# Two transformer layers on one core: the weights' preparation issued by Pool, and exponentials on VectorE in all heads of the first layer

## The chip, the cores and the metric

One core of a Trainium2 chip runs the whole program in a single launch. The metric is device time in microseconds (us); several timed runs give a median, and one further execution is recorded by the profiler. The engines are TensorE (PE, with its weight loads as PEld), VectorE (DVE), ScalarE (ACT), GpSimd (Pool) and SyncE (SP). Each works through its own instructions in order and waits on semaphores; SP, ACT and Pool can begin DMA transfers from their queues.

## The reference

Attention and a gated feed-forward block alternate, twice, with the same weights in both layers:

```
x: 2048 x 448, 16 heads of 28, feed-forward width 1792
for layer in 0, 1:
    q, k, v = layernorm(x) @ wqkv                      # per head 2048 x 28 each
    x = x + concat_h(softmax(q k^T * 28**-0.5) v) @ wo
    z = layernorm(x)
    x = x + (sigmoid(z @ w_gate) * (z @ w_up)) @ w_down
```

All inputs and the output are float32.

## The kernel before, in words

Every float32 matrix is cut into a high and a low float16 part, and products are sums of part products. In layer 0 the parts of `wqkv` are made at the start. The parts of `wo`, `w_gate`, `w_up` and `w_down` are made during the attention of layer 0 by the class `Prepare` (L715) and written to DRAM tensors `o_parts`, `gu_parts`, `dn_parts`; both layers load them from there afterwards.

**Attention** (`attend`, L831). The score matrix of a head, transposed, has 16 chunks of 128 keys by 4 blocks of 512 queries: 64 units of 128x512 per head, 1024 per layer. `score(g)` (L860) takes the next three units of the list `main`: TensorE writes their scores into a triple of PSUM banks (tile `sc`, L856; four matmuls per unit), and one ScalarE instruction at L871 turns all three into exponentials (tile `prob`, ring of six). This is called a group here. `mix` (L897, matmuls at L907) multiplies exponentials by the values into the accumulator `acc`, a PSUM bank that alternates with the head: `bank(h % 2, "acc")`. It goes chunk by chunk, each chunk in four quarters. When the last chunk of a head is mixed, `finish(h)` (L928) has VectorE copy the accumulator to `oraw` (L933), take the reciprocal of the denominators (L935), scale and cut into parts; SP then sends the parts to the tiles `ot` (L951, L953).

**Units aside.** The units in `side` are not in `main`. Their scores go into one PSUM bank of their own (tile `aside`), and VectorE computes their exponential with a polynomial of ten instructions (`score_aside`, L873, chain L881 to L890). The bank is that of the other accumulator: `bank(1 - h % 2, "aside")`, so it comes free when `oraw` of the previous head has been copied. In layer 0 only heads 10 to 15 have such units, two each (begun at chunks 4 and 9 of the head); in layer 1 all heads have two.

**Order.** It is written out by hand. The loop over groups (L986) emits `more(g)` (the next group, and at the third chunk of a head the loads of head `h + 2`: a memset by VectorE at L467 and six transfers by SP, L471 to L478), then a unit aside if one is due, then as many quarters of `mix` as `due` says. When a chunk `c` of the layer (0 to 255) has been mixed, `along(c)` (L919) may emit one step of the preparation.

**The preparation.** It has twelve tiles: one of `wo`, four of `w_down`, seven of `w_gate` with `w_up`. Twelve steps measure the tiles (VectorE sums squares, L773, L775), one step (`sizes`, L787) turns the sums into powers of two with a Pool reduction, twelve steps cut the tiles again (VectorE at L189 and L194) and the last one writes what is left. Each step first begins the read of the next tile (L171 to L174 in `load_rows`, or L744), then the write of the parts cut by the step before (L766), and then emits the VectorE work on its own tile. A gate/up tile needs six reads. All of these transfers are begun by SP. The tiles `raw`, `junk` and `pack` come from `big`, a first-in first-out list of free slots that the head operands `qp`, the outputs `ot` and others draw on too; a slot that is taken again makes its new writer wait for its old readers.

```
            if prepare and prepare.steps and c > 4 and c % 6 == 0:
                prepare.steps.popleft()()
```

So a step is emitted every six chunks, from chunk 6 to chunk 156, which is in head 9.

Of the kernel before, what the change touches and what calls it, by code (L numbers as in the profile page):

```python
# [12 lines left out]
BF16 = mybir.dt.bfloat16  # L13
F16 = mybir.dt.float16
# [5 lines left out]
P = 128  # L20
S = 2048
D = 448
H = 16
DH = 28
F = 1792
NT = S // P
NB = 4
# [61 lines left out]
def interleaved_layers(ctx: ExitStack, tc: tile.TileContext, x_in, wqkv, wo, w_gate, w_up,  # L89
                       w_down, out):  # L90
    nc = tc.nc
# [6 lines left out]
    big = Slots(spool, "s", N_SLOTS)  # L98
# [26 lines left out]
    x = cpool.tile([P, NT, D], F32, name="x")  # L125
# [40 lines left out]
    qrt.put(ind_f)  # L166


    def load_rows(dst, src, c0, n):

        nc.sync.dma_start(dst[:, 0:3, :],  # L171
                          src[0:384, c0:c0 + n].rearrange("(s p) n -> p s n", p=P))
        nc.sync.dma_start(dst[0:64, 3, :], src[384:448, c0:c0 + n])
        nc.sync.dma_start(dst[64:128, 3, :], src[384:448, c0:c0 + n])  # L174

    def split(hi, lo, raw):

        nc.scalar.copy(hi, raw)  # L178
        nc.vector.tensor_tensor(lo, raw, hi, op=ALU.subtract)  # L179
# [223 lines left out]
    o_parts = dpool.tile([P, 2, 4, D], F16, name="o_parts")  # L403
    gu_parts = dpool.tile([NF // 2, P, 2, 2, 4, 2 * P], F16, name="gu_parts")
    dn_parts = dpool.tile([4, P, 4, 2, D], F16, name="dn_parts")

    class WeightsQKV:
# [307 lines left out]
    class Prepare:  # L715


        def __init__(self):
            nc.vector.memset(sums[:, 3:7], 0.0)
            self.part = cpool.tile([P, 2], F32, name="part", tag="part", bufs=1)  # L720
            self.at = 0
            tiles = [("o", 0)] + [("d", j) for j in range(4)] + [("gu", j) for j in range(7)]
            self.read(*tiles[0])
            self.steps = deque()
            for do in (self.measure, self.split):
                for i, what in enumerate(tiles):
                    last = do == self.split and i == len(tiles) - 1
                    self.steps.append(lambda do=do, what=what, then=None if last else
                                      tiles[(i + 1) % len(tiles)]: self.step(do, what, then))
                if do == self.measure:  # L730
                    self.steps.append(self.sizes)
            self.steps.append(self.write)
            self.pack = None

        def read(self, kind, j):
            self.next = big.get("raw", [P, 2048])
            if kind == "o":
                load_rows(self.view(self.next, kind), wo, 0, D)
            elif kind == "gu":
                for i, w in enumerate((w_gate, w_up)):  # L740
                    load_rows(self.view(self.next, kind)[:, i], w, j * 2 * P, 2 * P)
            else:
                n = self.count(j)
                nc.sync.dma_start(self.view(self.next, kind)[:, 0:n, :],  # L744
                                  w_down[j * 512:j * 512 + n * P, :].rearrange(
                                      "(s p) n -> p s n", p=P))

        def count(self, j):
            return min(4, NF - 4 * j)
# [6 lines left out]
        def step(self, do, what, then):  # L756
            raw = self.next
            if then:
                self.read(*then)
            self.write()  # L760
            do(raw, *what)
            big.put(raw)

        def write(self):
            if self.pack:
                nc.sync.dma_start(*self.pack[0:2])  # L766
                big.put(self.pack[2])
                self.pack = None

        def add(self, m, v):  # L770
            junk = big.get("junk", [P, 2048], BF16)
            n = v.free_size()
            nc.vector.tensor_tensor_reduce(junk[:, 0:n], v, v, 1.0, sums[:, m:m + 1],  # L773
                                           op0=ALU.mult, op1=ALU.add, accum_out=self.part[:, 0:1])
            nc.vector.tensor_copy(sums[:, m:m + 1], self.part[:, 0:1])  # L775
            big.put(junk)

        def measure(self, raw, kind, j):
            if kind == "o":
# [16 lines left out]
        def split(self, raw, kind, j):  # L796
            v = self.view(raw, kind)
            if kind == "o":
                t = big.get("pack", [P, 2, 4, D], F16)
                scaled_split(t[:, 0], t[:, 1], v, 3, nc.vector)  # L800
                self.pack = (o_parts, t, t)
            elif kind == "gu":
                t = big.get("pack", [P, 2, 2, 4, 2 * P], F16)
                for w in range(2):
                    scaled_split(t[:, w, 0], t[:, w, 1], v[:, w], 4 + w, nc.vector)
                self.pack = (gu_parts[j], t, t)
            else:
                n = self.count(j)
                t = big.get("pack", [P, 4, 2, D], F16)
                scaled_split(t[:, 0:n, 0], t[:, 0:n, 1], v[:, 0:n], 6, nc.vector)  # L810
                self.pack = (dn_parts[j][:, 0:n], t[:, 0:n], t)

    class Outputs:

# [16 lines left out]
    def attend(layer, values, heads, last_values, gate, keep):  # L831
# [3 lines left out]
        prepare = None  # L835
# [4 lines left out]


        side = {}
        free_from = 10 if layer == 0 else 0
        for h in range(free_from, H):
            for at, kc, qb in ((4, 10, 3), (9, 15, 1)):
                side[(h * NT + at) * NB] = (h * NT + kc) * NB + qb
        main = [u for u in range(units) if u not in side.values()]
        groups = (len(main) + 2) // 3
# [70 lines left out]
        def along(c):  # L919
            nonlocal prepare  # L920
            if layer == 0 and c == 2:
                keep()
            if layer == 0 and c == 4:
                prepare = Prepare()
            if prepare and prepare.steps and c > 4 and c % 6 == 0:
                prepare.steps.popleft()()

        def finish(h):  # L928
            acc = accs.pop(h)
# [49 lines left out]


        quarters, i, done = 4 * total, 0, 0
        alone = main.index(free_from * NT * NB) // 3
        pace = (quarters + len(side) - 3 * alone) / (groups - alone)
        for g in range(2, groups + 3):
            more(g)
            x = g - 2.25  # L986
            due = int(3 * x if x < alone else 3 * alone + (x - alone) * pace)
            if g >= groups:
                due = 2 * quarters
            if begin:  # L990
# [68 lines left out]
    def gated(layer, first, wt, before_next):  # L1059
# [33 lines left out]
        for b, p in seq:  # L1093
# [113 lines left out]
```

## Time and profile before

| | |
|---|---|
| median of 3 runs | 2001.17 us (1999.59 to 2002.54) |
| the profiled execution: its time, its span | 2000.05 us, 1998.3 us |
| PE, DVE, ACT, POOL busy | 1965.6, 1003.4, 1167.3, 33.5 us |
| mean granted TensorE clock | 0.996 |
| exponentials of layer 0: first to last start at L871 | 126.1 to 591.8 us, 338 instructions |
| exponentials of layer 1: first to last start at L871 | 1124.1 to 1568.2 us, 331 instructions |

Busy time is what the profiler records for instructions; PE's is modelled and is near the whole span in every stage, so it does not tell where TensorE is short of time. The two stretches with exponentials take 910 of the 1998 us; between and after them come the projections and the feed-forward blocks, which the change does not touch.

### The profile page before, as it was taken

The numbers are of one execution on the slowest core, as the hardware profiler recorded it, in microseconds if no ns is written. First come the engines' busy times: TensorE is split into PE (matmuls) and PEld (weight loads), VectorE is DVE, ScalarE is ACT, GpSimd is POOL, SyncE is SP. The second block draws the span as 40 slices with busy tenths as digits, with TensorE's granted clock in tenths as the row PEclk, the third lists the DMA queues.
The fourth block names the chain that finished last, engine by engine and source line by source line (L and its number), as shares of the span: only waits on it lengthen the run. The fifth ranks groups of instructions, "written<-read, shape, count | busy, mean of one in ns | idle before, by whom it ended". The sixth has DMA issues, their size and how long they took to land. (4 is left out here: it accounts for less than half of the span.)

```text
span 1998.3 us, 48079 instructions
## 1 busy us (share of the span) xinstructions
PE 1965.6 (98%) x21549; PEld 1001.7 (50%) x21549; DVE 1003.4 (50%) x1551; ACT 1167.3 (58%) x1129; POOL 33.5 (2%) x76
## 2 busy tenths in 40 slices
PE   9999999979999999999999999999999999999999
PEld 4445555545554444444444555555555544444444
DVE  6634545477664323333255477677776732323222
ACT  5569999979981211121235699999999412121211
POOL 2000000000000000000000000000000000000000
PEclk9999999989999999999999999999999999999999
DMA  4563544751016101010234311111111250101000
GB/s 166 161 208 84 149 124 152 224 146 43 17 51 233 37 1 37 1 38 1 92 94 140 100 48 32 48 49 44 46 34 51 68 196 11 56 1 56 0 19 19
DMA packets 98633, 153.77 MB, mean 77 GB/s; under 512 B 9584, under 2 KB 79216, under 8 KB 95600
## 3 DMA queue, kind: packets, MB, share of 16 engines
q1 hardware_dynamic: 89728, 146.21, 23.9%
q10 hardware_dynamic: 8688, 4.36, 0.9%
q8 instruction: 173, 2.83, 0.6%
q14 instruction: 44, 0.36, 0.1%
HBM read 97.52 MB, written 45.68 MB: 72 GB/s over the span
## 5 line engine op out<-in xcount | busy, mean ns | idle before, releaser
L871 ACT ACTIVATE prob_s<-sc 128x1536 f32<-128x1536 f32 x669 | 898.4, 1562 | 15.4 <-PE sc L856 13.0
L907 PE MATMUL acc<-prob_s,val_s 128*32 128x256 f32 (+3 forms) x7938 | 568.1, 381 | 0.0
L856 PE MATMUL sc<-qp_s 114*32 114x512 f16 x8016 | 557.8, 380 | 3.2 <-ACT val_s L567 1.3
L1116 ACT ACTIVATE sig_q<-gate 128x512 f32<-128x512 f32 x112 | 60.8, 595 | 597.4 <-PE up L386 597.4
L856 PEld LDWEIGHTS <-qp_s 114*32 114x32 f16 x8192 | 247.6, 95 | 251.9 <-issue 142.8
L907 PEld LDWEIGHTS acc<-prob_s,val_s 128*32 128x32 f32 x7938 | 263.2, 110 | 155.1 <-issue 9.7
L1117 DVE SCALAR_TENSOR_TENSOR sig_q<-up,sig_q 128x512 f32<-128x512 f32 x112 | 72.1, 686 | 513.8 <-ACT sig_q L1116 513.8
L1080 PE MATMUL dnp<-dn_s,hhl_q 128*128 128x448 f16 x448 | 158.4, 354 | 0.0
L1081 PE MATMUL dnp<-dn_s,hhl_q 128*128 128x448 f16 x448 | 157.9, 352 | 0.0
L1082 PE MATMUL dnp<-dn_s,hhl_q 128*128 128x448 f16 x448 | 157.9, 352 | 0.0
L372 PE MATMUL qkp<-xhl_s,wqk_s 128*128 128x512 f16 x616 | 139.6, 379 | 2.6 <-ACT xhl_s L178 0.9
L379 PE MATMUL gate<-xhl_s,gu_s 128*128 128x512 f16 x336 | 127.3, 379 | 3.4 <-ACT xhl_s L178 2.5
L380 PE MATMUL gate<-xhl_s,gu_s 128*128 128x512 f16 x336 | 127.3, 379 | 1.4 <-DVE xhl_s L179 1.4
L381 PE MATMUL up<-xhl_s,gu_s 128*128 128x512 f16 x336 | 127.3, 379 | 0.0
L380 PE MATMUL up<-xhl_s,gu_s 128*128 128x512 f16 x336 | 127.3, 379 | 0.0
L379 PE MATMUL up<-xhl_s,gu_s 128*128 128x512 f16 x336 | 127.3, 379 | 0.0
L381 PE MATMUL gate<-xhl_s,gu_s 128*128 128x512 f16 x336 | 127.3, 379 | 0.0
L933 DVE COPY oraw_q<-acc 128x512 f32<-128x512 f32 x32 | 22.1, 692 | 179.1 <-PE acc L907 179.0
L935 DVE RECIPROCAL oden_q<-oden_q 128x512 f32<-128x512 f32 x32 | 107.3, 3353 | 1.1
L380 PEld LDWEIGHTS <-gu_s 128*128 128x128 f16 x672 | 65.7, 98 | 81.3 <-issue 3.9
L381 PEld LDWEIGHTS <-gu_s 128*128 128x128 f16 x672 | 65.7, 98 | 81.3 <-issue 2.5
L379 PEld LDWEIGHTS <-gu_s 128*128 128x128 f16 x672 | 65.7, 98 | 79.0 <-issue 1.7
(139 smaller groups left out, 1900.8 us busy)
## 6 DMA issues: line engine op xcount, KB each, us to landing
qp_s<-qk_scr SPq DMA_DIRECT2D x96, 224.0 KB
qk_scr<-qkhl_q SPq DMA_DIRECT2D x56, 256.0 KB
gu_s<-gu_parts SPq DMA_DIRECT2D x14, 1024.0 KB
xraw_s<-xt_scr SPq DMA_DIRECT2D x14, 768.0 KB
xt_scr<-xs_s SPq DMA_DIRECT2D x38, 224.0 KB
qp_s<-qk_scr SPq DMA_DIRECT2D x64, 112.0 KB
gu_parts<-pack_s SPq DMA_DIRECT2D x7, 1024.0 KB
raw_s<-in_B_w_down_dram SPq DMA_DIRECT2D x6, 896.0 KB
```

What stands on the lines that cost most here:

```text
L372: nc.tensor.matmul(pm, w, x, start=(i == 0), stop=(i == len(terms) - 1))
L379: nc.tensor.matmul(pm, wh(o, kt), blk.hi[:, kt, :], start=(kt == 0), stop=False)
L380: nc.tensor.matmul(pm, wh(o, kt), blk.lo[:, kt, :], start=False, stop=False)
L381: nc.tensor.matmul(pm, wl(o, kt), blk.hi[:, kt, :], start=False, stop=False)
L856: nc.tensor.matmul(ps[32 * j:32 * j + 32, :], hd.k[:, keys], hd.q[:, qb * W:(qb + 1) * W], start=True, stop=True, tile_position=(0, 32 * j))
L871: nc.scalar.activation(prob[:, 0:n, :], ps[:, 0:n, :], AF.Exp, scale=exp_scale)
L907: nc.tensor.matmul(acc[qb * VC:(qb + 1) * VC, s], v[:, kc % TB, h, :], probs[c * NB + qb][:, s], start=(kc == 0 and a == 0), stop=(kc == N ...
L935: nc.vector.reciprocal(den, den)
L1080: nc.tensor.matmul(pm, hl[:, 0, s], dw[:, 0, :], start=(f == 0), stop=False)
L1081: nc.tensor.matmul(pm, hl[:, 0, s], dw[:, 1, :], start=False, stop=False)
L1082: nc.tensor.matmul(pm, hl[:, 1, s], dw[:, 0, :], start=False, stop=(f == NF - 1))
L1117: nc.vector.scalar_tensor_tensor(sigs[a], pms[2 * a + 1], PS, sigs[a], op0=ALU.mult, op1=ALU.mult)
```

## The change

The reads and writes of the preparation are begun by Pool in place of SP. Its tiles come from two rings of their own, two slots for `raw` and two for `pack` and `junk`, taken from `big` at the start of the preparation and given back at its end. Its steps have due chunks: the measuring steps at chunks 6, 10, ... 50, `sizes` and the first cut at 54, the cuts at every sixth chunk up to 120, the last write at 126, in head 7. In layer 0 heads 0 to 8 get one unit aside each (begun at chunk 6 of the head, for key chunk 15), heads 9 to 15 two, as in layer 1. The pace of `mix` is worked out for the two parts.

```diff
-    def load_rows(dst, src, c0, n):
+    def load_rows(dst, src, c0, n, queue=nc.sync):
-        nc.sync.dma_start(dst[:, 0:3, :],
+        queue.dma_start(dst[:, 0:3, :],
...
     class Prepare:
-            self.at = 0
+            self.raws, self.packs = big.ring(2), big.ring(2)
             tiles = [("o", 0)] + [("d", j) for j in range(4)] + [("gu", j) for j in range(7)]
+            order = [(do, what) for do in (self.measure, self.split) for what in tiles]
...
+            at = 6
+            for i, (do, what) in enumerate(order):
+                then = order[i + 1][1] if i + 1 < len(order) else None
+                self.steps.append((at, lambda do=do, what=what, then=then:
+                                   self.step(do, what, then)))
+                at += 4 if do == self.measure else 6
+                if i == len(tiles) - 1:
+                    self.steps.append((at, self.sizes))
+            self.steps.append((at, self.end))
...
+        def along(self, c):
+            while self.steps and self.steps[0][0] <= c:
+                self.steps.popleft()[1]()
+
+        def end(self):
+            self.write()
+            big.free.extend(self.raws)
+            big.free.extend(self.packs)
...
-            self.next = big.get("raw", [P, 2048])
+            self.next = big.at(self.raws, "raw", [P, 2048])
             if kind == "o":
-                load_rows(self.view(self.next, kind), wo, 0, D)
+                load_rows(self.view(self.next, kind), wo, 0, D, nc.gpsimd)
...
         def write(self):
             if self.pack:
-                nc.sync.dma_start(*self.pack[0:2])
-                big.put(self.pack[2])
+                nc.gpsimd.dma_start(*self.pack)
                 self.pack = None
 
         def add(self, m, v):
-            junk = big.get("junk", [P, 2048], BF16)
+            junk = big.at(self.packs, "junk", [P, 2048], BF16)
...
-                t = big.get("pack", [P, 2, 4, D], F16)
+                t = big.at(self.packs, "pack", [P, 2, 4, D], F16)
...
     def attend(layer, values, heads, last_values, gate, keep):
-        free_from = 10 if layer == 0 else 0
-        for h in range(free_from, H):
-            for at, kc, qb in ((4, 10, 3), (9, 15, 1)):
+        both = 9 if layer == 0 else 0
+        for h in range(H):
+            for at, kc, qb in ((4, 10, 3), (9, 15, 1)) if h >= both else ((6, 15, 1),):
                 side[(h * NT + at) * NB] = (h * NT + kc) * NB + qb
...
-            if prepare and prepare.steps and c > 4 and c % 6 == 0:
-                prepare.steps.popleft()()
+            if prepare:
+                prepare.along(c)
...
-        alone = main.index(free_from * NT * NB) // 3
-        pace = (quarters + len(side) - 3 * alone) / (groups - alone)
+        few = both * NT * NB
+        turn = main.index(few) / 3
+        paces = (few + both) / max(turn, 1), (quarters + len(side) - few - both) / (groups - turn)
         for g in range(2, groups + 3):
             more(g)
             x = g - 2.25
-            due = int(3 * x if x < alone else 3 * alone + (x - alone) * pace)
+            due = int(min(x, turn) * paces[0] + max(x - turn, 0) * paces[1])
```

More of the change, by code (lines that the diff above doesn't have):

```diff
@@ L166, in interleaved_layers @@
     qrt.put(ind_f)
-    def load_rows(dst, src, c0, n):
[L171 to L174, printed above, removed]
+    def load_rows(dst, src, c0, n, queue=nc.sync):
+        queue.dma_start(dst[:, 0:3, :],
+                        src[0:384, c0:c0 + n].rearrange("(s p) n -> p s n", p=P))
+        queue.dma_start(dst[0:64, 3, :], src[384:448, c0:c0 + n])
+        queue.dma_start(dst[64:128, 3, :], src[384:448, c0:c0 + n])
     def split(hi, lo, raw):
@@ L720, in __init__ @@
             self.part = cpool.tile([P, 2], F32, name="part", tag="part", bufs=1)
-            self.at = 0
+            self.raws, self.packs = big.ring(2), big.ring(2)
             tiles = [("o", 0)] + [("d", j) for j in range(4)] + [("gu", j) for j in range(7)]
+            order = [(do, what) for do in (self.measure, self.split) for what in tiles]
             self.read(*tiles[0])
             self.steps = deque()
[L725 to L731, printed above, removed]
@@ L732, in __init__ @@
-            self.steps.append(self.write)
-            self.pack = None
+            at = 6
[6 more added lines that the diff above has]
+                    self.steps.append((at, self.sizes))
@@ L739, in read @@
             elif kind == "gu":
                 for i, w in enumerate((w_gate, w_up)):
-                    load_rows(self.view(self.next, kind)[:, i], w, j * 2 * P, 2 * P)
+                    load_rows(self.view(self.next, kind)[:, i], w, j * 2 * P, 2 * P, nc.gpsimd)
             else:
                 n = self.count(j)
-                nc.sync.dma_start(self.view(self.next, kind)[:, 0:n, :],
-                                  w_down[j * 512:j * 512 + n * P, :].rearrange(
-                                      "(s p) n -> p s n", p=P))
+                nc.gpsimd.dma_start(self.view(self.next, kind)[:, 0:n, :],
+                                    w_down[j * 512:j * 512 + n * P, :].rearrange(
+                                        "(s p) n -> p s n", p=P))
@@ L761, in step @@
             do(raw, *what)
-            big.put(raw)
         def write(self):
             if self.pack:
-                nc.sync.dma_start(*self.pack[0:2])
-                big.put(self.pack[2])
+                nc.gpsimd.dma_start(*self.pack)
                 self.pack = None
         def add(self, m, v):
-            junk = big.get("junk", [P, 2048], BF16)
+            junk = big.at(self.packs, "junk", [P, 2048], BF16)
             n = v.free_size()
@@ L775, in add @@
             nc.vector.tensor_copy(sums[:, m:m + 1], self.part[:, 0:1])
-            big.put(junk)
         def measure(self, raw, kind, j):
@@ L798, in split @@
             if kind == "o":
-                t = big.get("pack", [P, 2, 4, D], F16)
+                t = big.at(self.packs, "pack", [P, 2, 4, D], F16)
                 scaled_split(t[:, 0], t[:, 1], v, 3, nc.vector)
-                self.pack = (o_parts, t, t)
+                self.pack = (o_parts, t)
             elif kind == "gu":
-                t = big.get("pack", [P, 2, 2, 4, 2 * P], F16)
+                t = big.at(self.packs, "pack", [P, 2, 2, 4, 2 * P], F16)
                 for w in range(2):
                     scaled_split(t[:, w, 0], t[:, w, 1], v[:, w], 4 + w, nc.vector)
-                self.pack = (gu_parts[j], t, t)
+                self.pack = (gu_parts[j], t)
             else:
                 n = self.count(j)
-                t = big.get("pack", [P, 4, 2, D], F16)
+                t = big.at(self.packs, "pack", [P, 4, 2, D], F16)
                 scaled_split(t[:, 0:n, 0], t[:, 0:n, 1], v[:, 0:n], 6, nc.vector)
-                self.pack = (dn_parts[j][:, 0:n], t[:, 0:n], t)
+                self.pack = (dn_parts[j][:, 0:n], t[:, 0:n])
     class Outputs:
```

## The prediction

> **What bounds the kernel now.** I read the page's costliest groups first, then the waits, then a table by stage, then the timeline around the one stage that stands out.
>
> The largest group after the modelled matmuls is the exponential of a group of three units:
>
> ```profile
> L871 ACT ACTIVATE prob_s<-sc 128x1536 f32<-128x1536 f32 x669 | 898.4, 1562 | 15.4 <-PE sc L856 13.0
> ```
>
> 898.4 us over 669 instructions is 1.343 us per group. 338 belong to layer 0 and 331 to layer 1, and in both layers the starts follow each other by 1.343 us where nothing goes wrong. Layer 1 has units aside in all heads, layer 0 only from head 10, so TensorE and VectorE carry different loads at the same pace: ScalarE sets it. ScalarE waited 15.4 us in all, and 13.0 of that for scores. The table by stage (columns: length, busy us and instructions of PE, PEld, DVE, ACT, POOL, granted clock, DMA share, GB/s) shows where:
>
> ```profile
> 350.00:400.00 50.00, 50.00 (x904) 26.52 (x899) 24.41 (x24) 50.00 (x39) 0.00 (x0) 1.00 0.71 223
> 400.00:450.00 50.00, 39.67 (x698) 21.70 (x697) 37.61 (x45) 38.35 (x29) 0.00 (x0) 0.90 0.50 146
> 450.00:500.00 50.00, 50.00 (x924) 29.06 (x920) 34.99 (x49) 50.00 (x38) 0.00 (x0) 1.00 0.17 45
> 1150.00:1200.00 50.00, 50.00 (x928) 29.29 (x923) 35.40 (x50) 50.00 (x38) 0.00 (x0) 1.00 0.19 49
> ```
>
> ScalarE is busy throughout except in 400 to 450 us, where it and TensorE lose over ten. The timeline there, in order of time (start, length, engine, line, in brackets the idle time before and what ended it):
>
> ```profile
> 412.82 0.54 SPq L171 DMA_DIRECT2D raw_s<-in_B_w_gate_dram  x1
> ...
> 417.75 9.52 SPq L766 DMA_DIRECT2D gu_parts<-pack_s  x3
> 422.87 0.75 DVE L189 TENSOR_SCALAR pack_s<-raw_s,up 128x1024 f16<-128x1024 f32 x1 [9.60 <-DMA gu_parts<-pack_s]
> ...
> 427.40 1.76 DVE L467 MEMSET qp_s<- 18x2048 f16 x1 [0.48 <-issue]
> ...
> 429.20 0.69 DVE L933 COPY oraw_q<-acc 128x512 f32<-128x512 f32 x1
> ...
> 429.94 0.62 PE L856 MATMUL aside<-qp_s 114*32 114x512 f16 x4 [10.33 <-DVE oraw_q L933]
> ...
> 432.81 1.45 ACT L871 ACTIVATE prob_s<-sc 128x1536 f32<-128x1536 f32 x1 [11.39 <-PE sc L856]
> ```
>
> Read it from the bottom. ScalarE waits for scores, which stand behind the first unit aside of head 10 on TensorE. That unit needs the accumulator bank of head 9, whose copy (L933) stands on VectorE behind a memset and two cutting steps. The second step waited 9.60 us for a `pack` slot whose old parts SP began to write only at 417.75, after the next tile's six reads. The copies at 338.16, 368.12 and 402.52 us were late too (no idle time before them, against a rhythm of 28.5), but in heads without a unit aside nobody needs the bank for a whole head.
>
> **The change part by part.** The sum is made against the profiled 2000.05 us; the median of the runs is 1.12 us above it. About 0.2%, 4 us, is what a measurement can tell from no change.
>
> *Exponentials moved to VectorE.* Layer 0 has 9 + 14 = 23 units aside instead of 12. `main` shrinks from 1012 to 1001 units, groups from 338 to 334: 4 x 1.343 = **5.4 us** off ScalarE, on the path. Eleven more chains of 6.4 us (435.89 to 442.25) go to VectorE, which was busy 24.4 of 50 in 350 to 400: hidden, if the bank's copy comes in time (below). TensorE's matmuls are the same in number.
>
> *The stall.* The start after the gap comes 12.90 us after the one before, so 12.90 - 1.34 = **11.6 us** go if nothing is late in its place; two slow intervals behind it (1.66 and 1.51, at a granted clock of 0.90) give 0.5. From head 9 on no step of the preparation is left (the last write is due at chunk 126, head 7), so two units aside per head run as from 450 us on, where nothing stalls. A check: layer 1 takes 444.1 us for 330 intervals, 0.9 over 330 x 1.343; layer 0 takes 465.7 for 337, 13.1 over. The excess there is 11.6 + 0.5 and a start like layer 1's.
>
> *What is late next.* Now heads 1 to 8 have a unit aside while the preparation runs, each needing the copy of the head before. Begun at chunk 6 it leaves more room: in head 11 (chunk 4) the copy started at 457.62 and the matmuls at 459.75, 2.1 us on; two chunks are 2 x 28.2 / 16 = 3.5 more, so VectorE may be about 5.7 us late. It runs in order, so whatever makes a preparation step wait also holds the memset and the copy queued behind it, and TensorE's unit waits for that copy.
>
> The fullest stretch is head 2, with four gate/up measuring steps. VectorE's work per head (21 groups, 28.2 us) is 6.8 for `finish` (402.52 to 409.30), 6.4 for the chain, 1.8 memset, 4 x 3.0 measuring (194.51 to 197.53): 27.0. It fits with 1.2 to spare, so waits for reads decide. With two `raw` slots, read i+2 starts when measure i is done. Count from head 2's unit aside: the copy 5.7 earlier plus `finish` ends at 1.1, one measure 4.1, chain 10.5, next measure 13.5. There the last tile's read may start; it takes the issue time P of six transfers and 3.2 us to land (the last issue before 205.89 ended at 202.70), then 1.5 for the second half, 1.8 memset, 0.7 copy: 20.7 + P, needed at 28.2. So P up to 7.5 us, **1.25 us per transfer**, costs nothing.
>
> *Pool's issue.* No Pool transfer is in this trace, so I bound it. SP's same reads take 0.49 to 0.60, six in 3.4 us; the longest, 1.85, includes some wait. Pool's own slowest small operation is 0.975 us:
>
> ```profile
> L244 POOL TENSOR_TENSOR rs<-rs,nhalf 128x4 f32<-128x4 f32 (+1 forms) x16 | 15.6, 975 | 1.3
> ```
>
> Bounds: P = 3.0 (0.5 each) to 11.1 (1.85 each). I take 0.975, the same engine's row: P = 5.9, no cost. Cutting steps have 10.6 us for six reads and a write, 6.8 at this price. Behind these transfers Pool has only the reduction of `sizes`; its next work is the norm after the attention. Begun by Pool they cannot gain below zero: a landing earlier than needed moves no exponential.
>
> The Trainium skill speaks against the change here. "SBUF — State Buffer", section "SBUF: two separate sides", says that a transfer begun by GpSimd has its descriptors written by GpSimd itself, that fast VectorE modes shut it out, and that a transfer of some 620 ns then took some 3100. If each of six took that, the step would be an estimated 18.6 us, more than double the room. No run here shows a Pool transfer. What the rows allow is worked out under the rivals.
>
> *SP.* 98 reads and 12 writes of some 0.55 us, about 60 us of issue, leave its queue. Nothing on the path waits for it outside the stall; zero. If that cover were gone, late `qp` loads would show, but they have a whole head of room.
>
> *Slots.* Four slots fixed for rings leave fewer for `qp`, whose memset now waits for the scores of the head before last; those are past. Zero.
>
> Sum: 5.4 + 11.6 + 0.5 = **17.5 us**: 2001.2 - 17.5 = **1983.7 us**.
>
> **The rivals.** *A, the forecast:* Pool needs up to 1.25 us per transfer. 1981 to 1987. Chance 0.60.
>
> *B, small new stalls:* Pool needs 1.25 to 1.6. Eight reads in a row (seven gate/up tiles and `wo` again) have four chunks, 7.05 us, each; what P exceeds is summed eight times, less the 5.7 of room. At P = 8.5: 8 x 1.45 - 5.7 = 5.9, so 1989.6; up to 1997 at the far end. For it: VectorE is 27.0 of 28.2 full in head 2 and landings vary. Chance 0.17.
>
> *C, slower:* Pool needs 2 us, P = 12: 8 x 4.95 - 5.7 = 33.9, so 1983.7 + 33.9 = 2017.6. It decides from P = 10 on, 1.65 us per transfer, where the loss is 17.9 and the gain is gone. The place: copies of `acc` in heads 2, 3 and 7, behind steps that wait for reads. How it could be: Pool is held while VectorE runs its fast rows. Such rows are the 0.43 us ones for 128x512 (L882; L883 takes 0.69), the memset and L189; in a measuring head 4 x 0.43 + 1.76 = 3.5 us, 0.9 per step, P = 6.8, still under 7.5. So holding alone does not do it; Pool must also be slow by itself. Against: its small rows are all at or below 0.98. Chance 0.14. The skill's rule above, taken in full, is this rival and more.
>
> *D, TensorE sets the pace* once units aside are everywhere, and the 5.4 us are not gained: 1989.1. Against: layer 1 runs 1024 units in 331 groups at the same 1.343, denser than 334. Chance 0.05.
>
> *E, the change does not take the stall away*, because the copy before the first double head is late for another reason, and saves only ScalarE's work and part of the rest: about 1996 to 2001. Nothing in the profile is left to make it late once the preparation has ended. Chance 0.04.
>
> **How the numbers follow.** A, B and D are faster by more than 4 us, together 0.82. E I count as the same, 0.04. C is slower, 0.14. The range takes in A, B and D and leaves out C and E: 1980 (the runs spread by 1.5 either way) to 1997. A's own range is 1981 to 1987.
>
> **What would show it.** Right: 334 exponentials in layer 0, their starts 448 us from first to last, ScalarE busy 50 of 50 in every stretch from 150 to 550, granted clock 1.00 throughout; the copies of `acc` preceded by a wait for TensorE in most heads; Pool's reads under 1.25 us each. Wrong: TensorE's `aside` matmuls waiting for `oraw` in heads 2 to 4 or 7, VectorE's measuring or cutting waiting for reads just before (B, C), or intervals above 1.35 us with no wait for a copy (D). The forecast is wrong as a whole if a Pool transfer takes over 1.65 us.

## The result, and the profile after

The changed kernel takes 1983.59 us (median of 4 runs, 1981.17 to 1984.55), beside 2000.81 us for the kernel before. The ratio is 0.9912, 95% interval 0.9896 to 0.9928. Its profiled execution took 1983.66 us with a span of 1981.9; that of before took 2000.05. One run of the first experiment below came at a granted clock of 0.76 and took 3749 us; it is left out of that experiment's median.

The group of the exponentials and the table by stage, the views that the prediction began with (columns of the table: length, busy us and instructions of PE, PEld, DVE, ACT, POOL, granted clock, DMA share, GB/s):

```profile
L879 ACT ACTIVATE prob_s<-sc 128x1536 f32<-128x1536 f32 x665 | 893.2, 1532 | 4.9 <-DMA qp_s<-qk_scr 3.6
```

```profile
200.00:250.00 50.00, 50.00 (x912) 27.68 (x905) 43.64 (x66) 50.00 (x38) 16.80 (x27) 1.00 0.67 192
...
350.00:400.00 50.00, 50.00 (x928) 28.29 (x924) 31.16 (x39) 50.00 (x38) 0.53 (x1) 1.00 0.26 72
400.00:450.00 50.00, 50.00 (x904) 28.46 (x900) 35.59 (x48) 50.00 (x38) 0.00 (x0) 1.00 0.16 41
```

There are four groups fewer, and ScalarE's wait for scores no longer heads its idle time: what is left is the start, a wait for a `qp` load. The stretch 400 to 450 us, which had lost over ten us, is now like its neighbours, at a granted clock of 1.00. In 200 to 250 us, which begins in head 2, VectorE is busy 43.64 of 50 and Pool 16.80, and ScalarE still misses nothing.

The 16.4 us between the two profiled executions lie in layer 0. Its exponentials start over 449.8 us instead of 465.7, which is 15.9 less. The first of them starts 0.85 later; the stretch between the layers is 1.0 shorter (531.3 instead of 532.3) and what follows layer 1 is 0.3 shorter; layer 1 is unchanged (444.13 and 444.15).

The copies of `acc` show whether VectorE keeps up. In the timeline of head 2, the fullest one (start, length, engine, line, in brackets the idle time before and what ended it):

```profile
216.23 1.28 DVE L782 CUSTOM_DVE_ANT_0 junk_s<-raw_s,sums 128x1024 bf16<-128x1024 f32 x1 [1.16 <-DMA raw_s<-in_B_w_up_dram]
...
218.19 1.76 DVE L467 MEMSET qp_s<- 18x2048 f16 x1 [0.48 <-issue]
...
219.98 0.69 DVE L941 COPY oraw_q<-acc 128x512 f32<-128x512 f32 x1
...
223.97 0.40 PE L864 MATMUL aside<-qp_s 114*32 114x512 f16 x4
```

The copy stands, without a pause, behind the memset and the measuring of the sixth of the seven gate/up tiles, the last one measured in this head, whose second half had to be waited for. It ends at 220.7, and the unit aside that needs the bank runs at 223.97, without waiting: 3.3 us were left. In no head of layer 0 did an `aside` matmul wait for a copy. Of the waits in front of the copies themselves, the whole program shows

```profile
DVE oraw_q L941 <- PE acc L915: 179.4, 30, 12.9
```

so 30 of the 32 copies now come after a wait for TensorE: VectorE is there first. (Columns: total us, times, longest us.) The two others are those of heads 1 and 2 of layer 0.

Pool's transfers, one of these steps in its timeline, the three reads of its gate half (those of the up half follow, the last from 173.55 to 174.07):

```profile
170.43 0.76 POOL L171 DMA_DIRECT2D raw_s<-in_B_w_gate_dram  x1 [13.36 <-DVE sums L784]
171.19 0.54 POOL L173 DMA_DIRECT2D raw_s<-in_B_w_gate_dram  x1
171.72 0.54 POOL L174 DMA_DIRECT2D raw_s<-in_B_w_gate_dram  x1
```

All six take 3.6 us, hardly more than SP's 3.4. Not every tile goes so smoothly: of the fourteen gate/up tiles, Pool waited in three, 0.25 to 0.59 us, for the landing of an earlier read, and 4.2 us in a fourth, begun at 328.16, which took 8.0 us.

### The profile page after: what moved, and what is told of

Same layout as the page of the kernel before. It is cut to its first block, busy times and chain, and to the rows that moved or that the text cites. A ratio compares the mean times of both kernels' runs of the same rounds, so it can differ in the third digit from the quotient of the medians.

```text
span 1981.9 us, 48270 instructions
## 1 busy us (share of the span) xinstructions
PE 1960.6 (99%) x21557; PEld 1009.1 (51%) x21557; DVE 1069.5 (54%) x1661; ACT 1162.3 (59%) x1125; POOL 101.9 (5%) x186
## 3 DMA queue, kind: packets, MB, share of 16 engines
q1 hardware_dynamic: 67488, 111.80, 18.3%
q0 software_dynamic: 8448, 34.41, 5.7%
## 5 line engine op out<-in xcount | busy, mean ns | idle before, releaser
L879 ACT ACTIVATE prob_s<-sc 128x1536 f32<-128x1536 f32 x665 | 893.2, 1532 | 4.9 <-DMA qp_s<-qk_scr 3.6
L915 PE MATMUL acc<-prob_s,val_s 128*32 128x384 f32 (+3 forms) x7904 | 567.0, 381 | 0.0
L864 PEld LDWEIGHTS <-qp_s 114*32 114x32 f16 x8192 | 253.2, 95 | 227.8 <-issue 111.2
L915 PEld LDWEIGHTS acc<-prob_s,val_s 128*32 128x32 f32 x7904 | 264.8, 110 | 156.3 <-issue 12.9
L895 DVE SCALAR_TENSOR_TENSOR power_q<-power_q,expo_q 128x512 f32<-128x512 f32 x165 | 114.2, 692 | 5.6
L381 PEld LDWEIGHTS <-gu_s 128*128 128x128 f16 x672 | 65.7, 98 | 81.3 <-issue 2.5
L380 PEld LDWEIGHTS <-gu_s 128*128 128x128 f16 x672 | 65.7, 98 | 80.9 <-issue 3.5
```

What stands on the lines that cost most here:

```text
L380: nc.tensor.matmul(pm, wh(o, kt), blk.lo[:, kt, :], start=False, stop=False)
L381: nc.tensor.matmul(pm, wl(o, kt), blk.hi[:, kt, :], start=False, stop=False)
L864: nc.tensor.matmul(ps[32 * j:32 * j + 32, :], hd.k[:, keys], hd.q[:, qb * W:(qb + 1) * W], start=True, stop=True, tile_position=(0, 32 * j))
L879: nc.scalar.activation(prob[:, 0:n, :], ps[:, 0:n, :], AF.Exp, scale=exp_scale)
L895: nc.vector.scalar_tensor_tensor(p, p, c[k], y, op0=ALU.add, op1=ALU.mult)
L915: nc.tensor.matmul(acc[qb * VC:(qb + 1) * VC, s], v[:, kc % TB, h, :], probs[c * NB + qb][:, s], start=(kc == 0 and a == 0), stop=(kc == N ...
```

## The experiments

The changed kernel makes four edits: the queue (Pool instead of SP), the slots (rings instead of shared ones), the due chunks of the steps, and the units aside with their pace. The theory is that of the prediction: 5.4 us from ScalarE's shorter list, 12.1 from the stall, and Pool's issue for nothing up to about 1.25 us per transfer. The rivals: that one of the two gains is the other in disguise, that another of the edits carries the stall, and that the price of a transfer is not what decides. Edits are against the changed kernel unless said otherwise. "Layer 0" is the time from the start of its first exponential to that of its last: 465.7 us before, 449.8 after. It is read in the profiled execution, the time in all runs. The experiments ran on three chips, on which the kernel before took 2001.65 to 2003.11 us, so a difference of 2 us between times from different chips tells nothing.

**Only the stall.** The kernel before, with one constant changed:

```diff
-        free_from = 10 if layer == 0 else 0
+        free_from = 11 if layer == 0 else 0
```

> The kernel before with one constant changed: units aside in layer 0 begin at head 11 in place of head 10, two units fewer (10 in all, main 1014 units, still 338 groups). Theory (the stall is the accumulator bank of head 9, wanted by the first unit aside while its copy stands behind waiting cuts): head 9's late copy no longer holds anybody, the preparation is over before head 11, so 11.6 + 0.5 us go and no group is saved: 2001.2 - 12.1 = 1989. Rival (the gap at 420 us is made by something else, say the transfers or the granted clock): the gap stays, 2001; or it moves to head 11 at the same size.

1991.05 us, ratio to the kernel before 0.9932 (0.9909 to 0.9954). Still 338 groups, layer 0 454.8 us, and no later interval between exponentials above 1.63. The gap was there only because head 10's unit aside asked for a bank that a late VectorE had not emptied; a head later nothing is late. That is 10.9 us in layer 0, with a start that was 1.1 longer (its second interval, see the run on the start below), so 12.0 with equal starts, against 12.1 expected. The stall is shown as a thing by itself.

**Only the exponentials taken back.** No unit aside in heads 0 to 9, and two from head 10 on, with the pace of `mix` worked out to match; the preparation as in the changed kernel:

```diff
-        both = 9 if layer == 0 else 0
+        both = 10 if layer == 0 else 0
-            ... if h >= both else ((6, 15, 1),):
+            ... if h >= both else ():
```

> The changed kernel without the nine units of heads 0 to 8 and with two units from head 10 on: 12 units aside and 338 groups as before, the new preparation kept. Theory (ScalarE sets the pace): four groups more, 4 x 1.343 = 5.4 us above the changed kernel, 1989. Rival (TensorE sets the pace, or the units on VectorE cost what they save): same as the changed kernel, 1983.6.

1988.95 us (ratio 0.9926, 0.9900 to 0.9951), layer 0 454.6 us with 338 groups. Against the changed kernel that is 5.4 us in the time and 4.8 in layer 0, for four groups. (The two layers 0 differ in two more things: the changed kernel's second interval is 1.3 longer, and this run has one slow interval of 2.27 us near 249, 0.9 too long. Without both, the four groups are 5.2 us.) ScalarE's list is worth what its length says, so TensorE did not set the pace.

**The old preparation under the new units.** The kernel before with the changed kernel's units and pace, nothing else:

```diff
-        free_from = 10 if layer == 0 else 0
-        for h in range(free_from, H):
-            for at, kc, qb in ((4, 10, 3), (9, 15, 1)):
+        both = 9 if layer == 0 else 0
+        for h in range(H):
+            for at, kc, qb in ((4, 10, 3), (9, 15, 1)) if h >= both else ((6, 15, 1),):
```

> The units aside and the pace of the changed kernel, with the preparation of the kernel before (SP, shared slots, a step every six chunks). Theory (copies of the accumulator that are late behind the preparation become stalls as soon as a unit aside wants the bank; room 5.7 us with one unit per head, 2.1 with two): stalls before the units of heads 7, 8, 9 and 10, where before's copies were 7 to 14 us late, 20 us or more in place of 11.6, against 5.4 saved: 2000 to 2012. Rival (the preparation's order matters only at head 10, so the units alone give the gain): 1984 to 1990.

1991.34 us (ratio 0.9947, 0.9926 to 0.9968): the expectation was missed on the good side. One stall came, not several, at the first unit of head 9:

```profile
378.75 1.29 DVE L194 SCALAR_TENSOR_TENSOR pack_s<-raw_s,up,pack_s 128x1024 f16<-128x1024 f32 x1
...
389.98 1.76 DVE L467 MEMSET qp_s<- 18x2048 f16 x1 [9.95 <-DMA gu_parts<-pack_s]
...
391.77 0.69 DVE L933 COPY oraw_q<-acc 128x512 f32<-128x512 f32 x1
...
392.52 0.62 PE L856 MATMUL aside<-qp_s 114*32 114x512 f16 x4 [5.03 <-DVE oraw_q L933]
```

The same pattern as before, only that here the memset itself waits 9.95 us for a slot that a write on SP, begun at 384.55 behind six reads, has not let go. But the copies were less late than in the kernel before (358.9, 391.8 and 421.4 us instead of 368.1, 402.5 and 429.2), though the preparation's code is the same; VectorE's waits for cutting (L189) came to 7.0 us instead of 42.0. (Some 3 us of the difference in the copies are the quicker pace of the heads, 28.2 us instead of 28.6.) That the chains of the added units fill time in which VectorE used to wait is an argument; no run here shows it.

**The queue taken back.** All of the change, but SP begins the transfers:

```diff
-                load_rows(self.view(self.next, kind), wo, 0, D, nc.gpsimd)
+                load_rows(self.view(self.next, kind), wo, 0, D)
-                nc.gpsimd.dma_start(*self.pack)
+                nc.sync.dma_start(*self.pack)
```

(and the down and gate/up reads likewise.)

> The changed kernel with all transfers of the preparation begun by SP again; rings, schedule and units kept. Theory (the rings and the earlier schedule take the waits away, the queue matters less): within 4 us of the changed kernel, 1983 to 1988, with reads issued later behind loads and outputs. Rival (what counts is that SP is not held by the preparation and the preparation not by SP): reads and writes stand behind the outputs of each head in SP's queue, VectorE waits for them, copies come late and TensorE waits at units aside in heads 2 to 8: 1990 to 2010.

1984.37 us (ratio 0.9902, 0.9878 to 0.9926), layer 0 450.3 us. In the time it can't be told from the changed kernel; in the trace it can, by VectorE's and TensorE's waits in 130 to 440 us:

```profile
DVE pack_s L189 <- DMA dn_parts<-pack_s: 9.6, 2, 6.2
...
DVE pack_s L189 <- DMA gu_parts<-pack_s: 5.5, 2, 3.0
```

```profile
PE aside L864 <- DVE oraw_q L941: 1.8, 1, 1.8
```

Cutting waits 15.1 us for writes that stand in SP's queue (2.0 in the changed kernel); in all, VectorE waits 28.1 us for transfers of the preparation, against 11.9. It costs one stall of 1.8 us in head 7, where the copy of head 6 stands behind cuts that waited 4.13 us for a read and 2.98 for a write.

**The rings taken back.** Pool's queue kept, the slots again from `big`, shared with `qp`:

```diff
-            self.raws, self.packs = big.ring(2), big.ring(2)
-            self.next = big.at(self.raws, "raw", [P, 2048])
+            self.next = big.get("raw", [P, 2048])
-            junk = big.at(self.packs, "junk", [P, 2048], BF16)
+            junk = big.get("junk", [P, 2048], BF16)
-                t = big.at(self.packs, "pack", [P, 2, 4, D], F16)
+                t = big.get("pack", [P, 2, 4, D], F16)
```

(and `big.put` after the last use of each.)

> The changed kernel with its raw, junk and pack tiles taken from the shared list of slots again and given back after each step; Pool's queue, schedule and units kept. Theory (own tiles are needed: in the shared list VectorE's memset for the next head operands waits for a write of parts in the slot, and the copy behind it): some stalls at units aside in heads 4 to 8, where parts are written, 1985 to 1995. Rival (the queue alone does it, slots do not matter): 1983.6.

1982.03 us (ratio 0.9903, 0.9886 to 0.9919), layer 0 448.5 us, no stall. The theory that `qp` and the preparation would take slots from each other fell: VectorE waited once for a slot, 1.1 us, and never for a read. The rings are not needed. With them VectorE waited 9.7 us for reads while measuring, in the same stretch; the tight copy of head 2 above stands behind two of these waits (1.91 and 1.16). With shared slots the copies of heads 1 and 2 come after waits for TensorE again (3.05 and 0.86).

**Queue and due chunks, apart.** With shared slots and the same units in all, the two remaining edits form a square. SP with the new due chunks:

> The changed kernel with SP's queue and the shared list of slots, so that of the new preparation only the schedule is left (12 steps every four chunks, 12 every six, done in head 7). Theory (the queue of Pool is what keeps VectorE from waiting, as VectorE waits 1.1 us for transfers of the preparation with Pool and shared slots, some 22 us with SP and rings; the early end only takes the waits out of the heads with two units): stalls of 2 to 8 us at units aside of heads 4 to 8, 1985 to 1992. Rival (the early end alone removes the stall): 1982 to 1984.

1986.94 us (ratio 0.9916, 0.9899 to 0.9933), layer 0 453.7 us. The old wait for a slot is there, ahead of the copy of head 5, which holds up nobody; VectorE is then late, and ahead of the copy of head 6 a cut waits 3.6 us for a read. Behind that one stands a stall of 2.3 us, in head 7:

```profile
DVE qp_s L467 <- DMA gu_parts<-pack_s: 9.0, 1, 9.0
...
DVE pack_s L189 <- DMA raw_s<-in_B_w_gate_dram: 4.6, 2, 3.6
```

```profile
PE aside L864 <- DVE oraw_q L941: 2.3, 1, 2.3
```

Pool with the old due chunks, a step at every sixth:

```diff
-                at += 4 if do == self.measure else 6
+                at += 6
                 if i == len(tiles) - 1:
                     self.steps.append((at, self.sizes))
+                    at += 6
```

> The changed kernel with the shared list of slots and a step of the preparation every six chunks again, to chunk 156 in head 9; Pool's queue and the units kept. Theory (with Pool's queue VectorE does not wait and the copies come in time whatever the pace): no gap over 2 us, 1981 to 1985. Rival (the early end is what counts): the unit of head 9 at its chunk 4 waits 5 us or so for a copy behind two cuts, as with the old preparation, 1988 to 1991.

1982.43 us (ratio 0.9894, 0.9877 to 0.9910), layer 0 448.5 us, no interval over 2.21:

```profile
DVE qp_s L467 <- DMA o_parts<-pack_s: 3.5, 1, 3.5
...
DVE qp_s L467 <- DMA gu_parts<-pack_s: 2.2, 1, 2.2
```

The runs on one table, with those of the two sections before (rings with the old due chunks were not run):

| time, us (layer 0) | old due chunks | new due chunks | new due chunks, rings |
|---|---|---|---|
| SP | 1991.34 (455.3) | 1986.94 (453.7) | 1984.37 (450.3) |
| Pool | 1982.43 (448.5) | 1982.03 (448.5) | 1983.59 (449.8) |

Two of these have the longer start told of below. With the second interval at 2.20 us in all, layer 0 is 455.3, 452.5 and 450.3 with SP, and 448.5 three times with Pool. The times agree in their order but are less sharp: the 4.4 us between the first two of SP come from two chips, their 95% intervals overlap, and the profiled execution of the second, at 1990.29, was the slowest of its four.

Read along the rows, the due chunks and the rings bring something only with SP's queue: 2.8 and 2.2 us of layer 0, nothing with Pool's. Read down, the queue brings 6.8, 4.0 and 1.8 us of layer 0 (8.9, 4.9 and 0.8 in the time). So Pool's queue by itself is enough to let VectorE keep up. It is not the only way: due chunks and rings together, with SP's queue, leave only 1.8 us. Begun by Pool, the old order of steps would have done, though only just: in that run the copy of head 9 started at 416.0 and ended at 416.7, and the first unit of head 10, which needs the bank, ran at 416.9.

**Dearer transfers.** To test the price at which Pool's issue begins to cost, each gate/up tile is read in 12 and in 20 smaller transfers instead of six:

```diff
+        if queue is nc.gpsimd:
+            rows = src[0:384, c0:c0 + n].rearrange("(s p) n -> p s n", p=P)
+            for r in (0, 64):
+                queue.dma_start(dst[r:r + 64, 0:3, :], rows[r:r + 64])
+            for r in (0, 32, 64, 96):
+                r0 = 384 + r % 64
+                queue.dma_start(dst[r:r + 32, 3, :], src[r0:r0 + 32, c0:c0 + n])
+            return
```

(With 20, each of the three slabs is also read by itself.)

> The changed kernel with each gate/up tile read in 12 transfers in place of 6 (halves of the partitions; the same bytes). Pool's time for a read goes from 3.7 us (170.43 to 174.07) to about 6.7 by its rows of 0.52 to 0.78. Theory (issue time costs nothing up to 7.5 us per tile, then it is summed over the eight reads in a row): no loss, or under 2 us, 1983 to 1986. Rival (issue time is never on the path): the same; rival (there is no room left, as the copy of head 2 is already late): 8 x 3 = 24 us more, 2008.

1987.44 us (ratio 0.9928, 0.9910 to 0.9946), a little over the expectation. Back to back a tile takes 6.4 us (182.20 to 188.62), but Pool also waits for landings, as the timeline of another tile, begun at 205.03, shows:

```profile
209.53 0.54 POOL L177 DMA_DIRECT2D raw_s<-in_B_w_up_dram  x1
211.44 0.51 POOL L177 DMA_DIRECT2D raw_s<-in_B_w_up_dram  x1 [1.38 <-DMA raw_s<-in_B_w_gate_dram]
213.78 0.50 POOL L177 DMA_DIRECT2D raw_s<-in_B_w_up_dram  x1 [1.82 <-DMA raw_s<-in_B_w_gate_dram]
214.82 0.50 POOL L177 DMA_DIRECT2D raw_s<-in_B_w_up_dram  x1 [0.55 <-DMA raw_s<-in_B_w_gate_dram]
```

That tile took 10.3 us from its first issue to the end of its last, so the next read began only at 215.35, and the unit of head 3 waited 2.6 us for the copy of head 2. A tile's price is not its transfers alone: the seven tiles that are measured took 6.4 to 10.3 us, 7.7 in the mean with the waits. The run does not place the end of the room nearer than between P = 6.4 and that, and the 7.5 of the prediction lies there.

> The changed kernel with each gate/up tile read in 20 transfers (blocks of 64 and 32 rows; the same bytes). Pool's time for a read becomes about 20 x 0.53 = 10.6 us, above 7.05 per step. Theory: seven gate/up reads in a row lose 3.55 us each less 5.7 of room, 19 us, and the cuts (11.2 against 10.6 of room) up to 4 more: 2003 to 2008, the stalls standing at units aside of heads 2 and 3. Rival (issue time is never on the path): 1984.

2018.23 us, ratio 1.0084 (1.0066 to 1.0101): slower than before the change. A tile takes 10.05 us (181.13 to 191.18). The longest stall in the timeline, its stage, and VectorE's longest wait in 130 to 440 us:

```profile
243.33 0.62 PE L873 MATMUL aside<-qp_s 114*32 114x512 f16 x4 [17.46 <-DVE oraw_q L950]
```

```profile
200.00:250.00 50.00, 32.54 (x572) 17.93 (x564) 30.05 (x47) 31.15 (x24) 44.40 (x89) 0.83 0.47 121
```

```profile
DVE pack_s L198 <- DMA raw_s<-in_B_w_gate_dram: 20.5, 3, 9.9
```

Pool is busy 44.40 of 50, VectorE has fallen to 30.05 from 43.64, and ScalarE with TensorE behind it. TensorE's stalls stand in heads 2, 3 and 7 (3.1, 17.5 and 9.9 us), the heads that the prediction named. The amount does not fit in all: the steps that measure lost 20.6 us, about the 19 expected, but those that cut lost 9.9 and not up to 4, and the time is 10 us beyond what was expected.

**The later start.** In the changed kernel the first exponential starts 0.85 us later than before, and the second interval is 3.48 us instead of 2.20. Do the reads that Pool begins during the projections delay the `qp` loads? A tiny Pool product of an exponential of chunk 5, ahead of the preparation, moves the first read from 121.33 to 140.36 us:

```diff
+                hold = cpool.tile([P, 1], F32, name="hold", tag="hold", bufs=1)
+                v = probs[min(probs)][:, 0:1]
+                nc.gpsimd.tensor_tensor(hold, v, v, op=ALU.mult)
                 prepare = Prepare()
```

> The changed kernel with Pool held before the first read of the preparation until an exponential of chunk 5 is done (one tiny Pool product that reads it), so that the first two reads start at about 136 us in place of 121.3. Theory (the first exponentials are late by 0.85 us and the third by 1.3 more because these reads share the transfer engines with the operands of heads 0 and 1): first start back near 126.1, second interval 2.2 in place of 3.5, about 2 us faster, 1981.5. Rival (the start is late for another reason): 1983.6, start as in the changed kernel; or later reads make the copy of head 2 later and cost up to 2 us.

1983.46 us (ratio 0.9906, 0.9892 to 0.9920), second interval 3.38, first exponential at 127.84, later still. The first exponential in this run's timeline:

```profile
127.84 2.79 ACT L879 ACTIVATE prob_s<-sc 128x1536 f32<-128x1536 f32 x2 [3.83 <-DMA qp_s<-qk_scr]
```

The theory fell: with no weight read before 140 the load of `qp` is as late (in the changed kernel the first exponential starts at 126.94 after a wait of 3.40 for it). The second interval is 3.3 to 3.8 in the changed kernel and in the runs from head 11, with 12 reads, with the late read, and with SP and the new due chunks, and about 2.2 in the others, on both sides of every edit. Its cause stays open. That it is 3.30 in the first experiment, the kernel before with one constant changed, says that neither Pool nor the new preparation is needed for it.

**More units aside.** Is there more to move? Shared slots as above, and three units aside in every even head where there were two:

```diff
+            two = ((4, 10, 3), (9, 15, 1)) if h % 2 else ((4, 10, 3), (8, 15, 1), (11, 15, 2))
-            for at, kc, qb in ((4, 10, 3), (9, 15, 1)) if h >= both else ((6, 15, 1),):
+            for at, kc, qb in two if h >= both else ((6, 15, 1),):
```

> The changed kernel with the shared list of slots and three units aside in place of two in every second head (heads 10, 12, 14 of layer 0, all even heads of layer 1): 333 and 328 groups in place of 334 and 331. Theory (ScalarE still sets the pace): 4 x 1.343 = 5.4 us less, 1977. Rival (TensorE is the bound from here on: 1024 units at twice 0.65 / 3 = 0.433 us are 444 us, what layer 1 takes already): layer 1 stays at 444 us, 1981 to 1983; or VectorE is too full and copies come late, 1985 and more.

1984.57 us (ratio 0.9909, 0.9893 to 0.9926): no gain. Four groups left ScalarE, three of them in layer 1, and layer 1 took 443.4 us instead of 444.1. The page's group, and the table's rows for layer 1, first of the changed kernel, then of this run:

```profile
L880 ACT ACTIVATE prob_s<-sc 128x1536 f32<-128x1536 f32 x661 | 891.6, 1491 | 3.3 <-PE sc L865 2.3
```

```profile
1150.00:1500.00 350.00, 350.00 (x6424) 205.03 (x6420) 253.87 (x352) 350.00 (x262) 0.00 (x0) 1.00 0.16 43
1150.00:1500.00 350.00, 350.00 (x6516) 225.02 (x6511) 289.19 (x411) 349.60 (x259) 0.00 (x0) 1.00 0.17 43
```

The mean interval in layer 1 rose from 1.346 to 1.356, so layer 1 gave 0.7 us for three groups where ScalarE's list says 4.0. ScalarE no longer sets the pace: its exponentials got shorter (1491 ns on the page instead of 1532) while the interval grew, so they overlap less, and in the stretch shown it misses 0.4 us. VectorE was not late: no `aside` matmul waited for a copy. That leaves TensorE, whose matmuls are the same in number and have to pass in fewer intervals, and 443.4 us is what the rival said of it. This is an argument from the time; the trace shows no wait for scores inside layer 1, only 2.3 us at the starts of the layers. The move to VectorE ends about where the change stands.

No version beat the changed kernel beyond what the runs can tell. Pool with shared slots, in both orders, came lowest (1982.0 and 1982.4 against 1983.6); the start of layer 0 accounts for 1.3 of that.

## Why the prediction was right

**The exponentials, 5.4 us:** shown, by taking the early units back (5.4 in the time; 4.8 in layer 0, 5.2 with the two late intervals taken out).

**The stall, 11.6 and 0.5 us:** shown, by one constant in the kernel before. The mechanism was as read: a late copy of `acc` behind steps of the preparation, paid for only in a head that needs the bank. That the two terms add up is less simple than the sum has it: with the units and the pace alone, layer 0 was 10.4 us shorter, 5.4 for the groups and 5.0 of the stall, and the new preparation took away the other 7.

**The sum:** 17.5 expected against the time before; 16.4 between the two profiled executions, 17.2 between the medians. The start of layer 0 took back 2.1 (0.85 later, and 1.3 in the second interval) and 1.3 came from the stretch between the layers and the end, neither of them in the sum. That the predicted time was met within 0.2 us is in part luck: these two partly cancel. With equal starts layer 0 is 17.2 us shorter, which is what the sum was about. One slip stands in the ranges: at 1.6 us per transfer, P = 9.6, the sum of B gives 8 x 2.55 - 5.7 = 14.7, so 1998.4 and not 1997; the forecast does not rest on it.

**The room of 5.7 us:** in an undisturbed head the copy started at 161.34 and the unit at 167.55, 6.2 us apart. Head 2 was the fullest, as worked out; there they were 4.0 apart, so it used 2.2 of them. The counting through head 2 came out nearly step by step. Its unit aside ran at 195.76, and the read that decides began 12.9 us later (13.5 in the prediction):

```profile
208.69 0.78 POOL L171 DMA_DIRECT2D raw_s<-in_B_w_gate_dram  x1 [5.59 <-DVE sums L784]
```

The six reads took 3.6 us, the second half could be measured 3.9 after them (3.2), and the copy ended 24.9 us after the unit of head 2, where the prediction's 20.7 + P gives 24.3 for P = 3.6. The unit of head 3 ran at 28.2, as counted.

**Pool's issue:** mis-sized, with no effect on the time. I took 0.975 us per transfer from a small Pool operation, so P = 5.9; the gate/up reads took 0.61 in the mean, P = 3.6. The lower row, SP's, was the near one. The rule of the Trainium skill that was weighed there ("SBUF — State Buffer", section "SBUF: two separate sides") is not borne out at these loads: beside a VectorE busy 43.64 of 50, with memsets and cutting among it, Pool's reads of gate/up tiles kept 0.52 to 0.90, and the longest of all, one of `w_down`, was 1.38. Which of VectorE's rows are the fast modes that the rule means, no run here tells.

**The point at which Pool would cost:** the mechanism and the heads were right, the size was not. At P = 10.05 the rule of eight steps gave a loss of 18.3 against the changed kernel, so a time near that of before; measured were 34.6. For the steps that measure, which the rule is about, it was near: they lost 20.6. Those that cut had no term in the loss and lost 9.9: at that price six reads have become 20, and a tile and its write fill their 10.6 us alone, with no time left for the landing. The remaining 4 us lie in the exponentials around the stalls (an interval of 20.1 us where TensorE waited 17.5). Between the two runs with dearer reads (3.8 lost at 6.4, 34.6 at 10.05) a straight line puts the loss of 17.5, the break-even, at about P = 8, counted without waits, an estimate, in place of 10.

**SP's relief, zero, and the slots, zero:** on top of the other edits both are small, as said: with equal starts, layer 0 is 1.8 us longer with SP's queue (0.8 in the time) and the same with shared slots. But zero was no reading of the cause. I counted the queue as a price to be paid and credited the end of the stall to the steps being done by head 7. The table above shows that this is not needed: with the new units in place the queue by itself takes 6.8 us of layer 0 away, the due chunks by themselves 2.8, rings after that 2.2, and on top of the queue neither brings anything. What the transfers left behind on SP was a place in line. In the kernel before, SP's queue shows it just ahead of the six reads of 412.82 and the write of 417.75:

```profile
409.33 3.45 SPq L951 DMA_DIRECT2D ot_s<-ohl_q  x4
```

The reads stand behind the outputs of a head, which VectorE's `finish` had only just made, the write that frees a slot behind the reads, and VectorE behind the write. In Pool's queue a write has only the preparation's own transfers before it.

**TensorE as the pace (D)** was wrong at 334 groups and, by the argument above, right in layer 1 at 328, closer than I had thought.

## What to carry to other kernels

When a step stalls behind a queue in order, look at what the stalled transfer frees and who is queued behind the one that needs it: moving the transfers to another engine's queue can be worth more than rearranging when they are due (here 6.8 us against 2.8 of layer 0). A late step costs only where something needs its result soon, so before mending the lateness, try starting the consumer one round later. After taking work off the bounding engine, check the pace of the next one: here layer 0 could give up four groups, and layer 1, already at 331, not three more.

## What the runs showed of the hardware beyond what was expected

Pool begins transfers about as fast as SP: 0.52 us for a read of 64 rows, 0.77 for the three-slab read of 128 rows, 0.58 for a write, with 5.3 us (median) from issue to landing for the reads. On the page its transfers form a queue of another kind, "software_dynamic", with 8448 packets and 34.41 MB.

Pool's issues wait at times for the landings of earlier ones: in a few tiles of six reads (0.25 to 0.59 us, once 4.2), and more with twelve (1.38, 1.82 and 0.55 us in the lines above). So many small transfers cost more than their issue time. And the granted clock is lower where TensorE stalled: 0.83 in the stage with the stall of 17.5 us, 1.00 in the same stage of the changed kernel.
